# GpSimd in written order, and transposes of r, v and x moved from TensorE to the DMA crossbar from tile 10 on

## The chip, the cores and the metric

The kernel runs on one core of a Trainium2 chip. The metric is the device time of one execution in microseconds (us). The fast executions of one kernel on one core agree within about 1.5 per cent here, so each comparison below is of medians over several runs, taken beside runs of the kernel before on the same chip.

## The reference

A linear recurrence per head (seq 768, 8 heads of 40, batch 4), followed by a mixing block. Cut to what matters:

```python
for t in range(S):                       # the recurrence
    y[t]  = r[t] @ state
    Sa    = state @ a[t]
    state = state * w[t] - outer(Sa, b[t]) + outer(v[t], k[t])
# x = y as (batch, seq, 320)
theta  = x @ w_theta
zr, zi = x * cos(theta), x * sin(theta)
u      = x + w_tok_r @ zr + w_tok_i @ zi
out    = u + relu(u @ w_ch)
```

Inputs and output are float32. The kernel works in chunks ("tiles") of 128 time steps: 24 tiles, 6 per batch entry, numbered 0 to 23.

## The kernel before: the parts that matter

The loop is software-pipelined. Step i computes the recurrence of tile i, while tile i+4 is loaded, i+2 is prepared and i+1 is scored; theta of tile i-1 is made in the same step. Each tile has six loads of 160 KB, all issued from SyncE (SP).

```python
for dst, ap in ((q.w, w), (q.kb[:, 0], k), (q.kb[:, 1], b),
                (q.a, a), (q.rv[:, 0], r), (q.rv[:, 1], v)):
    nc.sync.dma_start(out=dst, in_=src(ap))                    # load(i)

# prep_rv: cast r and v to bf16, one after the other
nc.gpsimd.tensor_copy(out=q.rvb[:, j, :, 0:D], in_=q.rv[:, j])
# prep_csi: k and b times invW;   prep_cse: a times Wi (the tile ah)
nc.gpsimd.tensor_tensor(out=q.kbh[:, j, :, 0:D], in0=q.kb[:, j], in1=q.invW[:, 0], op=ALU.mult)

def tr_rv(i):                            # eight 128x128 transposes on TensorE, one copy out of PSUM
    q = tiles[i]
    pt = tile_of(ps_sm, [128, 1024], BF16, "sm")
    transpose4(pt[:, 0:512], q.rvb[:, 0])
    transpose4(pt[:, 512:1024], q.rvb[:, 1])
    q.rvT = tile_of(trs, [128, 2, 512], BF16, "rvT")
    evac(out=q.rvT.rearrange("p a b -> p (a b)"), in_=pt)

def out_xt(i):                           # three transposes of x, for theta
    tiles[i].xT = x_transpose(x_t[i % (2 * NCH)], f"xT{i % NCH}")

for i in range(N):
    nxt(load, i + 4)
    ...                                  # recurrence of tile i
    if i > 0:
        out_y(i - 1)                     # writes x of tile i-1
    nxt(prep_csi, i + 2)
    nxt(prep_cse, i + 2)
    ...
    if i > 0:
        out_xt(i - 1)
    ...
    nxt(prep_rv, i + 2)
    for m in yrows:
        moe_y(*m)
    nxt(tr_rv, i + 2)
    if i > 0:
        moe_theta(i - 1)                 # reads xT of tile i-1
    sc_lams(i, i + 1)                    # reads rvT of tiles i and i+1
```

The order in the source isn't the order on the engines: a scheduler orders each engine's instructions by what it reckons will be ready first, and leaves in written order only those that are marked with `keep_in_program_order`. The orders are fixed when the program is built. In the kernel before, GpSimd's casts and products and SP's DMAs aren't marked.

Of the kernel before, what the change touches and what calls it, by code (L numbers as in the profile page):

```python
# [10 lines left out]
BF16 = mybir.dt.bfloat16  # L11
AF = mybir.ActivationFunctionType
ALU = mybir.AluOpType
# [5 lines left out]
def kernel(  # L19
# [14 lines left out]
    nc = tc.nc  # L34
    B, H, S, D = r.shape
    C = 128
    NCH = S // C
    DM = H * D
# [21 lines left out]
    nc.vector.memset(pi2_col, math.pi / 2)  # L60

    NB = 4

    def padded(name, shape, n, pads):
        ts = [consts.tile(shape, BF16, name=f"{name}_{i}") for i in range(n)]
        for i, t in enumerate(ts):
            to_zero.append((i, pads(t)))
        return ts
# [7 lines left out]
    ah_t = padded("ah", [128, H, 64], 2, last24)  # L76
    kb_t = padded("kb", [128, 2, H, 64], NB, last24)
    rv_t = padded("rv", [128, 2, H, 64], NB, last24)
    nu_t = padded("nu", [128, H, 64], 2, last24)
    gt_t = padded("gt", [128, G, 2, 64], 2, last24)  # L80
    x_t = padded("x", [128, 3 * 128], 2 * NCH, lambda t: t[:, DM:])
# [6 lines left out]
    trs = ctx.enter_context(tc.tile_pool(name="trs", bufs=3))  # L88
    scs = ctx.enter_context(tc.tile_pool(name="scs", bufs=2))
    sml = ctx.enter_context(tc.tile_pool(name="sml", bufs=2))  # L90
    xp = ctx.enter_context(tc.tile_pool(name="xp", bufs=2))
# [8 lines left out]
    def evac(out, in_):  # L100
        if busy_act[0]:
            nc.vector.tensor_copy(out=out, in_=in_)  # L102
        else:
            nc.scalar.copy(out=out, in_=in_)  # L104
# [4 lines left out]
    def tile_of(pool, shape, dt, tag):  # L109
        return pool.tile(shape, dt, name=tag, tag=tag)  # L110
# [3 lines left out]

    tiles = [T() for _ in range(B * NCH)]

    def load(i):
        q = tiles[i]
        bi, ci = divmod(i, NCH)

        def src(ap):
            return ap[bi, :, ci * C:(ci + 1) * C, :].rearrange("h t d -> t h d")
        q.w = tile_of(raw, [128, H, D], FP32, "raw_w")
        q.a = tile_of(raw, [128, H, D], FP32, "raw_a")
        q.kb = tile_of(raw, [128, 2, H, D], FP32, "raw_kb")
        q.rv = tile_of(raw, [128, 2, H, D], FP32, "raw_rv")
        for dst, ap in ((q.w, w), (q.kb[:, 0], k), (q.kb[:, 1], b),
                        (q.a, a), (q.rv[:, 0], r), (q.rv[:, 1], v)):
            nc.sync.dma_start(out=dst, in_=src(ap))  # L129
# [7 lines left out]
    def prep_rv(i):  # L137
        q = tiles[i]
        q.rvb = rv_t[i % NB]
        for j in range(2):  # L140
            if i < 2:
                nc.scalar.copy(out=q.rvb[:, j, :, 0:D], in_=q.rv[:, j])
            else:
                nc.gpsimd.tensor_copy(out=q.rvb[:, j, :, 0:D], in_=q.rv[:, j])

    reload = [False]

    def prep_csi(i):
        q = tiles[i]
        csi = tile_of(ps_sm, [128, 512], FP32, "sm")  # L150
        nc.tensor.matmul(csi[:, 0:DM], lhsT=ntri_inc, rhs=q.lw[:, :, 0:D],
                         start=True, stop=True)
        if reload[0]:
            ln_exp_again()
            reload[0] = False
        q.invW = tile_of(exps, [128, 1, H, D], FP32, "invW")
        tc.keep_in_program_order(nc.scalar.activation(  # L157
            out=q.invW.rearrange("p o h d -> p (o h d)"), in_=csi[:, 0:DM],
            func=AF.Exp))
        q.kbh = kb_t[i % NB]  # L160
        for j in range(2):
            (nc.vector if i < 2 else nc.gpsimd).tensor_tensor(  # L162
                out=q.kbh[:, j, :, 0:D], in0=q.kb[:, j], in1=q.invW[:, 0],
                op=ALU.mult)

    def prep_cse(i):
        q = tiles[i]
        cse = tile_of(ps_sm, [128, 512], FP32, "sm")
        nc.tensor.matmul(cse[:, 0:DM], lhsT=tri_exc, rhs=q.lw[:, :, 0:D],
                         start=True, stop=True)  # L170
        nc.tensor.matmul(cse[:, DM:DM + 8], lhsT=ident,
                         rhs=off_diag.rearrange("p g c -> p (g c)"),
                         start=True, stop=False, skip_group_check=True)
        for g in range(G):
            nc.tensor.matmul(cse[:, DM + 2 * g:DM + 2 * g + 2],
                             lhsT=q.lw[:, 2 * g:2 * g + 2, :].rearrange(
                                 "p a b -> p (a b)"),
                             rhs=ones2, start=False, stop=True,
                             skip_group_check=True)
        q.Wi = tile_of(exps, [128, DM + 8], FP32, "Wi")  # L180
        tc.keep_in_program_order(nc.scalar.activation(
            out=q.Wi, in_=cse[:, 0:DM + 8], func=AF.Exp))
        q.ah = ah_t[i % 2]
        (nc.vector if i < 2 else nc.gpsimd).tensor_tensor(
            out=q.ah[:, :, 0:D], in0=q.a,
            in1=q.Wi[:, 0:DM].rearrange("p (h d) -> p h d", h=H), op=ALU.mult)

    def transpose4(dst, src):
        for g in range(G):
            nc.tensor.transpose(out=dst[:, g * 128:(g + 1) * 128],  # L190
                                in_=src[:, 2 * g:2 * g + 2, :].rearrange(
                                    "p a b -> p (a b)"),
                                identity=ident)
# [15 lines left out]

    def tr_rv(i):  # L210
        q = tiles[i]
        pt = tile_of(ps_sm, [128, 1024], BF16, "sm")
        transpose4(pt[:, 0:512], q.rvb[:, 0])
        transpose4(pt[:, 512:1024], q.rvb[:, 1])
        q.rvT = tile_of(trs, [128, 2, 512], BF16, "rvT")
        evac(out=q.rvT.rearrange("p a b -> p (a b)"), in_=pt)
# [117 lines left out]
    def out_nut(i):  # L334
        q = tiles[i]
        pt = tile_of(ps_sm, [128, 1024], BF16, "sm")
        transpose4(pt[:, 0:512], q.nu)
        q.nuT = tile_of(trs, [128, 512], BF16, "nuT")
        nc.scalar.copy(out=q.nuT, in_=pt[:, 0:512])  # L339
# [22 lines left out]
                                op=ALU.mult)  # L362

    def out_xt(i):
        tiles[i].xT = x_transpose(x_t[i % (2 * NCH)], f"xT{i % NCH}")

    def x_transpose(src, tag):
        pt = tile_of(ps_sm, [128, 1024], BF16, "sm")
        for kt in range(3):
            nc.tensor.transpose(out=pt[:, kt * 128:kt * 128 + 128],  # L370
                                in_=src[:, kt * 128:kt * 128 + 128], identity=ident)
        dst = tile_of(xp, [128, 3, 128], BF16, tag)
        evac(out=dst.rearrange("p a b -> p (a b)"), in_=pt[:, 0:384])
        return dst
# [81 lines left out]
    def ln_exp_again():  # L456
        tc.keep_in_program_order(nc.scalar.preload_act_table_set(LN_EXP))
# [15 lines left out]
    def moe_y(bi, j):  # L473
        yp = tile_of(ps_sm, [128, 512], FP32, "sm")
        y_part(yp[:, 0:DM], bi, j, range(NT), True, True)
        y_evac(yp[:, 0:DM], bi, j)

    def moe_ut(bi, j):
        q = tiles[bi * NCH + j]
        q.uT = x_transpose(u_t[(bi * NCH + j) % 3], "uT")  # L480
# [10 lines left out]
    N = B * NCH  # L491
    nc.scalar.preload_act_table_set(LN_EXP)

    def nxt(f, i):
        if i < N:
            f(i)
# [7 lines left out]
    for i in range(4):  # L504
        load(i)
# [19 lines left out]
    for i in range(N):  # L525
        bi, ci = divmod(i, NCH)
        yrows = rows_at.get(i, [])
        sines = ci == 4 or (ci == 1 and bi > 0)
        nxt(load, i + 4)
        rec_x0(i)  # L530
        nxt(tr_a, i + 1)
        nxt(tr_kb, i + 1)
        rec_nu(i)
        if i > 0:
            out_y(i - 1)
        nxt(prep_csi, i + 2)
        nxt(prep_cse, i + 2)
        nxt(sc_psiphi, i + 1)
        out_nut(i)
        rec_gt(i)  # L540
        nxt(ev_phi, i + 1)
        if i > 0:
            out_xt(i - 1)
        nxt(prep_ln, i + 3)
        if sines:
            due = (bi, (0, 1, 2)) if ci == 4 else (bi - 1, (3, 4, 5))
            moe_sines(*due)
            z_due += [(due, m) for m in range(3)]
            reload[0] = True
            busy_act[0] = True  # L550
        for m in prev:
            moe_ch(*m)
        nxt(prep_rv, i + 2)
        for m in yrows:
            moe_y(*m)
        nxt(tr_rv, i + 2)
        if i > 0:
            moe_theta(i - 1)
        sc_lams(i, i + 1)
        rec_gd(i)  # L560
        for m in yrows:
            moe_ut(*m)
        busy_act[0] = False
        if i == 0:
            moe_weights()
        if 3 <= i < NCH + 3:
            wtok_load(i - 3)
        if 6 <= i < NCH + 6:
            wtok_trans(i - 6)
        for e in z_due[:1 if ci not in (2, 3) and i < N - 1 else 3]:  # L570
            moe_z(*e)
            z_due.remove(e)
        prev = yrows
# [59 lines left out]
```

## Time and profile before

| | before |
|---|---|
| time, median of 3 runs | 247.59 us (245.44 to 248.49) |
| profiled span, mean granted TensorE clock | 244.9 us, 0.967 |
| step 12 to 21, mean | 8.36 us |
| DMA moved | 30.81 MB |

Two groups of lines of the page of the kernel before are needed beside those that the prediction shows. They are the busy time of the engines with its share of the span and the number of instructions, and the DMA queue of SP with packets, MB and the share of the 16 engines' time.

```profile
PE 206.4 (84%) x3368; PEld 161.5 (66%) x3368; DVE 188.4 (77%) x289; ACT 157.7 (64%) x301; POOL 119.7 (49%) x184
...
q1 hardware_dynamic: 153216, 27.54, 62.2%
```

TensorE (PE) is the fullest engine, and VectorE (DVE) comes next. SP's queue already takes 62% of the 16 DMA engines' time, most of it in the first 130 us, where the slices of the page show the DMA at 9 tenths.

### The profile page before, as it was taken

To read this page: it belongs to the slowest core of one execution; us is meant where nothing else is said; L and a number is where in the kernel's file an instruction comes from. 1 tells how busy PE (TensorE), PEld (TensorE's weight loads), DVE (VectorE), ACT (ScalarE), POOL (GpSimd) and SP (SyncE) were. 2 spreads that over 40 slices of the span, in tenths; PEclk is the share of its full clock that TensorE was granted. 3 is DMA by queue.
4 is the path that set the end of the run, shared out by engine and by line. 5 is a ranking of instruction groups with operands and counts; after the bars stand their busy time and mean duration, and the time that the engine had idled before them with its cause. 6 is when DMAs were issued, how large, how long until landed. Compare 5 with 4: busy or idle time off the path is not lost.

```text
span 244.9 us, 8109 instructions
## 1 busy us (share of the span) xinstructions
PE 206.4 (84%) x3368; PEld 161.5 (66%) x3368; DVE 188.4 (77%) x289; ACT 157.7 (64%) x301; POOL 119.7 (49%) x184
## 2 busy tenths in 40 slices
PE   1476899974299699989999999989999999989992
PEld 0354578753277588767787778777877778666750
DVE  6387799987069979898889978997899878755063
ACT  2394677896056885687668866887688737625230
POOL 3009556537558759356545835584447340514100
PEclk9999999999569979999999999999999999999997
DMA  7999998999999999999979987654100000111012
GB/s 132 175 190 155 172 186 146 181 191 181 174 186 176 177 189 165 158 157 181 183 147 172 169 164 127 128 111 96 44 4 31 27 29 3 54 56 54 3 53 107
DMA packets 155684, 30.81 MB, mean 126 GB/s; under 512 B 150400, under 2 KB 155648, under 8 KB 155648
## 3 DMA queue, kind: packets, MB, share of 16 engines
q1 hardware_dynamic: 153216, 27.54, 62.2%
q0 software_dynamic: 2432, 2.77, 7.4%
q8 instruction: 26, 0.43, 0.8%
q14 instruction: 10, 0.08, 0.1%
HBM read 29.13 MB, written 3.93 MB: 135 GB/s over the span
## 4 chain that ended last, share of the span: by engine, by line
PE 52%; ACT 12%; DMA 10%; DVE 7%; POOL 7%; issue 6%; SPq 5%; POOLq 0%; ACTq 0%; DVEq 0%
PE sm L463 11%; PE sm L190 9%; PE sc L222 7%; PE sm L418 6%; SPq L129 5%; DMA raw_rv<-in_v_dram 5%; DVE lamu L230 3%; ACT cs L453 3%; DMA raw_rv<-in_r_dram 2%; DVE lamv L230 2%; PE sm L370 2%; PE sc L463 2%; PE sm L357 2%; ACT L453 2%; DMA raw_kb<-in_k_dram 2%
## 5 line engine op out<-in xcount | busy, mean ns | idle before, releaser
L230 DVE TENSOR_TENSOR lamv<-sc,mask_p 128x1024 bf16<-128x1024 f32 x24 | 29.3, 1223 | 9.7 <-PE sc L222 9.5
L230 DVE TENSOR_TENSOR psi<-sc,mask_p 128x1024 bf16<-128x1024 f32 x24 | 29.4, 1224 | 5.4 <-PE sc L222 4.8
L463 PE MATMUL sm<-zi,wtok_i 128*128 128x320 bf16 x120 | 33.1, 299 | 0.0
L463 PE MATMUL sm<-zr,wtok_r 128*128 128x320 bf16 x120 | 33.1, 299 | 0.0
L104 ACT COPY rvT<-sm 128x1024 bf16<-128x1024 bf16 x18 | 18.2, 1011 | 19.1 <-PE sm L190 19.0
L230 DVE TENSOR_TENSOR lamu<-sc,mask_p 128x1024 bf16<-128x1024 f32 x24 | 29.2, 1215 | 0.3 <-PE sc L222 0.3
L230 DVE TENSOR_TENSOR phi<-sc,mask_n 128x1024 bf16<-128x1024 f32 x24 | 29.1, 1214 | 0.0
L162 POOL TENSOR_TENSOR kb_92<-raw_kb,invW 128x320 bf16<-128x320 f32 x12 | 10.1, 865 | 26.0 <-ACT invW L157 26.0
L201 DVE COPY kbT<-sm 128x1024 bf16<-128x1024 bf16 x24 | 16.4, 683 | 8.0 <-PE sm L190 8.0
L208 ACT COPY aT<-sm 128x512 bf16<-128x512 bf16 x24 | 14.2, 590 | 9.2 <-PE sm L190 8.7
L339 ACT COPY nuT<-sm 128x512 bf16<-128x512 bf16 x24 | 14.1, 587 | 9.0 <-PE sm L190 9.0
L463 PEld LDWEIGHTS <-wtok_r 128*128 128x128 bf16 x144 | 14.0, 98 | 6.0 <-issue 0.8
L463 PEld LDWEIGHTS <-wtok_i 128*128 128x128 bf16 x144 | 14.0, 97 | 5.6
L222 PE MATMUL sc<-aT,kbT 64*128 64x128 bf16 x384 | 16.1, 229 | 0.0
L357 PEld LDWEIGHTS <-lamu 128*128 128x128 bf16 x192 | 13.4, 98 | 3.2 <-DVE lamu L230 3.1
L162 POOL TENSOR_TENSOR kb_93<-raw_kb,invW 128x320 bf16<-128x320 f32 x12 | 10.1, 860 | 10.3 <-ACT invW L157 10.3
L281 ACT ACTIVATE nx<-sm 128x320 bf16<-128x320 f32 x24 | 10.7, 444 | 6.4 <-PE sm L277 6.3
L432 ACT COPY th<-sm 128x320 f32<-128x320 f32 x24 | 10.3, 429 | 6.5 <-PE sm L418 6.4
L354 PEld LDWEIGHTS <-lamv 128*128 128x128 bf16 x192 | 14.0, 97 | 0.6 <-issue 0.5
L418 PE MATMUL sm<-wch,uT 128*128 128x320 bf16 x72 | 13.4, 299 | 1.2 <-ACT invW L157 0.6
L104 ACT COPY uT<-sm 128x384 bf16<-128x384 bf16 x18 | 8.5, 482 | 8.3 <-PE sm L370 8.3
L347 PE MATMUL sm<-gd,rvT 128*128 128x80 bf16 x80 | 13.1, 200 | 0.4 <-DVE gd L102 0.4
(334 smaller groups left out, 664.2 us busy)
## 6 DMA issues: line engine op xcount, KB each, us to landing
raw_w<-in_w_dram SPq DMA_DIRECT2D x24, 160.0 KB, 3.9
raw_kb<-in_k_dram SPq DMA_DIRECT2D x24, 160.0 KB, 3.9
raw_kb<-in_b_dram SPq DMA_DIRECT2D x24, 160.0 KB, 3.9
raw_a<-in_a_dram SPq DMA_DIRECT2D x24, 160.0 KB, 4.1
raw_rv<-in_r_dram SPq DMA_DIRECT2D x24, 160.0 KB, 3.9
raw_rv<-in_v_dram SPq DMA_DIRECT2D x24, 160.0 KB, 3.9
out_dram<-oo SPq DMA_DIRECT2D x24, 160.0 KB, 1.8
wtok_row_r<-in_moe_w_tok_r_dram POOLq DMA_DIRECT2D x6, 192.0 KB, 4.2
```

What stands on the lines that cost most here:

```text
L104: nc.scalar.copy(out=out, in_=in_)
L162: (nc.vector if i < 2 else nc.gpsimd).tensor_tensor(out=q.kbh[:, j, :, 0:D], in0=q.kb[:, j], in1=q.invW[:, 0], op=ALU.mult)
L190: nc.tensor.transpose(out=dst[:, g * 128:(g + 1) * 128], in_=src[:, 2 * g:2 * g + 2, :].rearrange("p a b -> p (a b)"), identity=ident)
L201: nc.vector.tensor_copy(out=q.kbT.rearrange("p a b -> p (a b)"), in_=pt)
L208: nc.scalar.copy(out=q.aT, in_=pt[:, 0:512])
L222: nc.tensor.matmul(P[:, p, g, :], lhsT=lhs[rows(p), g * 128:(g + 1) * 128], rhs=rhs[rows(p), g * 128:(g + 1) * 128], start=True, stop=True)
L230: nc.vector.tensor_tensor(out=s.rearrange("p a b c -> p (a b) c"), in0=P.rearrange("p a b c -> p (a b) c"), in1=mask.to_broadcast([128, 2 ...
L339: nc.scalar.copy(out=q.nuT, in_=pt[:, 0:512])
L354: nc.tensor.matmul(o, lhsT=q.lamv[:, p, g, :], rhs=q.kbh[:, 0, h, 0:D], start=first, stop=False, skip_group_check=True)
L357: nc.tensor.matmul(o, lhsT=q.lamu[:, p, g, :], rhs=q.kbh[:, 1, h, 0:D], start=False, stop=True, skip_group_check=True)
L418: nc.tensor.matmul(dst, lhsT=lhs[:, kt, :], rhs=rhs[:, kt, :], start=kt == 0, stop=kt == 2)
L463: nc.tensor.matmul(yp, lhsT=wtok[nm][:, sb, j * 128:(j + 1) * 128], rhs=z[:, sb], start=start and n == 0, stop=stop and n == 2 * len(sbs) - 1)
```

## The change

The intent has two parts. GpSimd's casts and products stay in written order, so that a cast waiting for its load can't stand in front of products whose data is there. And TensorE, which bounds the steady part, loses eleven transposes a step: from tile 10 on, r and v (rvT) and x (xT) are transposed by DMA, issued from SP. Beside this, tr_rv moves from two tiles ahead to one, and the two casts of ScalarE in tiles 0 and 1 are marked to stay in written order too (cut from the diff).

```diff
+    XBAR = 10
+    def on_pool(ins, i=2):
+        if i >= 2:
+            tc.keep_in_program_order(ins)
... (prep_rv, prep_csi, prep_cse: the GpSimd instruction is wrapped in on_pool)
-                nc.gpsimd.tensor_copy(out=q.rvb[:, j, :, 0:D], in_=q.rv[:, j])
+                on_pool(nc.gpsimd.tensor_copy(out=q.rvb[:, j, :, 0:D],
+                                              in_=q.rv[:, j]))
...
     def tr_rv(i):
         q = tiles[i]
+        if i >= XBAR:
+            q.rvT = tile_of(trs, [128, 2, 512], BF16, "rvT")
+            nc.sync.dma_start_transpose(
+                out=q.rvT.rearrange("p a (g t) -> p (a g) t", t=128),
+                in_=q.rvb.rearrange("p a h d -> p (a h d)"))
+            return
...
     def out_xt(i):
+        if XBAR <= i < N - 1:
+            tiles[i].xT = tile_of(xp, [128, 3, 128], BF16, f"xT{i % NCH}")
+            nc.sync.dma_start_transpose(out=tiles[i].xT, in_=x_t[i % (2 * NCH)])
+            return
...
+        if 2 <= i + 1 < N:
+            tr_rv(i + 1)
         for m in prev:
             moe_ch(*m)
         nxt(prep_rv, i + 2)
         for m in yrows:
             moe_y(*m)
-        nxt(tr_rv, i + 2)
```

More of the change, by code (lines that the diff above doesn't have):

```diff
@@ L141, in prep_rv @@
             if i < 2:
-                nc.scalar.copy(out=q.rvb[:, j, :, 0:D], in_=q.rv[:, j])
-            else:
-                nc.gpsimd.tensor_copy(out=q.rvb[:, j, :, 0:D], in_=q.rv[:, j])
+                tc.keep_in_program_order(
+                    nc.scalar.copy(out=q.rvb[:, j, :, 0:D], in_=q.rv[:, j]))
+            else:
+                on_pool(nc.gpsimd.tensor_copy(out=q.rvb[:, j, :, 0:D],
+                                              in_=q.rv[:, j]))
     reload = [False]
@@ L161, in prep_csi @@
         for j in range(2):
-            (nc.vector if i < 2 else nc.gpsimd).tensor_tensor(
+            on_pool((nc.vector if i < 2 else nc.gpsimd).tensor_tensor(
                 out=q.kbh[:, j, :, 0:D], in0=q.kb[:, j], in1=q.invW[:, 0],
-                op=ALU.mult)
+                op=ALU.mult), i)
     def prep_cse(i):
@@ L183, in prep_cse @@
         q.ah = ah_t[i % 2]
-        (nc.vector if i < 2 else nc.gpsimd).tensor_tensor(
+        on_pool((nc.vector if i < 2 else nc.gpsimd).tensor_tensor(
             out=q.ah[:, :, 0:D], in0=q.a,
-            in1=q.Wi[:, 0:DM].rearrange("p (h d) -> p h d", h=H), op=ALU.mult)
+            in1=q.Wi[:, 0:DM].rearrange("p (h d) -> p h d", h=H), op=ALU.mult), i)
     def transpose4(dst, src):
```

## The prediction

> **What bounds the kernel now.** I read the slices of the page first, then busy time by stretches, then the waits and the chain of waits around the one large hole, then the timeline of the steady part. The slices (40 of 6.1 us each) split the run:
>
> ```profile
> PE   1476899974299699989999999989999999989992
> PEclk9999999999569979999999999999999999999997
> DMA  7999998999999999999979987654100000111012
> ```
>
> DMA is full up to about 130 us and idle after 165. PE has one hole in the 11th slice (59 to 66 us); in the slices next to it the granted clock is 5 and 6 tenths. From 83 us on PE is full. Two stretches matter:
>
> ```profile
> 59.00:66.00 7.00, 0.40 (x4) 0.40 (x5) 1.39 (x2) 0.25 (x1) 4.30 (x7) 0.66 1.04 179
> 119.30:194.50 75.20, 72.56 (x1248) 58.00 (x1249) 67.21 (x92) 57.67 (x110) 42.38 (x60) 1.00 0.56 107
> ```
>
> The columns are length, then busy us of PE, weight loads, VectorE, ScalarE, GpSimd, then clock, DMA share, GB/s. In the first, nothing runs but GpSimd and the DMA. The second is nine steps of the loop (the negated x, nx, of tile 12 starts at 119.3, that of tile 21 at 194.5), so 8.36 us a step. PE is busy 72.56 of 75.20 and VectorE 67.21: **PE bounds this part, VectorE is next with 7.47 us a step**, ScalarE needs 6.4 and GpSimd 4.7.
>
> The hole is made by GpSimd's order. Its timeline there:
>
> ```profile
> 54.44 0.45 POOL L144 CAST rv_97<-raw_rv 128x320 bf16<-128x320 f32 x1 [3.72 <-DMA raw_rv<-in_r_dram]
> ...
> 62.65 0.45 POOL L144 CAST rv_94<-raw_rv 128x320 bf16<-128x320 f32 x1 [2.64 <-DMA raw_rv<-in_r_dram]
> 63.06 1.67 POOL L162 TENSOR_TENSOR kb_93<-raw_kb,invW 128x320 bf16<-128x320 f32 x2
> 64.69 0.86 POOL L184 TENSOR_TENSOR ah_89<-raw_a,Wi 128x320 bf16<-128x320 f32 x1
> ```
>
> The longest wait of PE in the view of waits (total, times, longest):
>
> ```profile
> PE sm L190 <- POOL ah_89 L184: 6.9, 1, 6.9
> ```
>
> Buffers go by tile number modulo 4, so rv_94 belongs to tile 8 and kb_93 to tile 7. The scheduler had placed the cast of r of tile **8** ahead of k, b and a of tile **7**, and that cast waited for its load until 62.65. What tile 7 needed had long been there: its invW was computed at 55.55 and its Wi at 55.89 (ScalarE's timeline), and its a was the load issued just before its r, whose cast began at 54.44. PE asked for ah of tile 7 from 58.7 and got it at 65.6.
>
> **What the Trainium skill says.** "TensorE: Matmul & The Clock Gate", Part 1, says that an idle window of about 3.4 us brings TensorE's clock to half and that sustained work brings it back. The trace agrees: after the 6.9 us hole the clock reads 0.84 over 66 to 83 us. "VectorE: DVE Perf Modes", section The three transpose paths, gives 390 ns for a 128x128 bf16 transpose on TensorE and 1309 ns by the DMA crossbar. The first is the time of one alone: in this trace eight in a row cost 56 ns each (below). "DMA: Bandwidth & Descriptors", Latency and other measured facts, gives 261 GB/s for a DMA transpose with a non-contiguous middle dimension and 350 to 400 when contiguous; no run so far shows one. Its section Issuing engines are not separate DMA queues says that all DMAs interleave on the same 16 engines; here loads of 160 KB take 3.9 us to land although one is issued every 0.8 us or so, hence some five are in flight, and a transpose issued in the full stage joins that queue.
>
> **The change, part by part.**
>
> *1. GpSimd in written order.* In each step this is k and b times invW, a times Wi, the casts of r and v of the same tile, then DMA issues and the products with cos and sin. This is also the order in which SP issues the loads (w, k, b, a, r, v), so a cast that waits for its load holds back only work whose data comes later still. No work is added. For tile 7: its k, b and a products could start when invW is there, 56.0, and take 1.67 + 0.82 = 2.5 us, so ah is ready at about 58.5, just when PE asks (58.7). The hole of 6.9 us closes. Tile 6 shows the same in small: its casts of rv waited until 46.13, its products came at 48.20, and PE's timeline has a gap of some 1.8 us there. The clock: 17 us at 0.84 instead of 1.0 are up to 2.7 us of lost array time, of which perhaps half lies on the path. The sum is 6.9 + 1.8 + 1.3 = 10. Against this, the DMA is full there and sets a new floor: a of tile 8 is issued at 54.90 and lands some 4 us later, so tile 8's products can end at about 61.5, where they now end at 71.4. The next loads come every 7 us or so, faster than a step of 8. So the loads don't take the gain back, but each part of it has to pass through steps that are no longer idle. I take **8 us**.
>
> *2. r and v transposed by DMA, tiles 10 to 23 (14 tiles).* PE loses eight transposes a tile. Their price is read from one row of the steady part:
>
> ```profile
> 174.90 0.61 PE L190 MATMUL sm<-ident,rv_94 128*128 128x128 bf16 x8
> ...
> L104 ACT COPY rvT<-sm 128x1024 bf16<-128x1024 bf16 x18 | 18.2, 1011 | 19.1 <-PE sm L190 19.0
> ```
>
> The last of the eight takes its modelled 0.22, so (0.61 - 0.22) / 7 = 0.056 us each, and 8 x 0.056 = 0.45 us a tile. The copy out of PSUM disappears with it: 1.01 us of ScalarE, or 0.69 of VectorE in the six that fall beside the sines.
>
> *3. x transposed by DMA, tiles 10 to 22 (13 tiles).* Three transposes, 3 x 0.056 = 0.17 us of PE, and a ScalarE copy of 0.48 us.
>
> Together PE gets 0.62 us a step, ScalarE 1.5 us, and one PSUM buffer of the four is asked for twice less often. Steps 9 to 22, some 13 steps: 13 x 0.62 = 8 us at most. VectorE's floor of 7.47 us (about 7.3 without its share of the rvT copies) stops a step at 0.9 to 1.0 us below today's 8.36, so it does not forbid the 0.62, but it gets close, and the chain of a step also passes over ScalarE and VectorE. I count 0.45 us for 13 steps, **6 us**.
>
> *4. What it costs.* 14 x 256 KB + 13 x 96 KB = 4.8 MB of extra transfer; at the skill's 261 GB/s an estimate of 19 us of full DMA, against loads that run short of work from 130 us on. The time to landing matters more. For rvT there is room: the cast comes a whole step before its scores. For xT there is little: x of tile 17 is written at 171.55 to 172.04 and its theta product starts at 175.34, so 3.3 us. After 130 us an unhindered DMA fits (stores here land in 1.8 us). In steps 11 to 14 the queue is full and a landing of 4 to 6 us would leave PE waiting 1 to 2 us a step, unless the schedule puts theta later. SP also issues in order: a transpose that waits for its cast or its x holds back the loads behind it, but by then the loads run two to three tiles ahead. I charge **2 us** in all.
>
> *5. tr_rv one step later.* For tiles 2 to 9, PE transposes r and v of the next tile, not of the one after. That asks for data a step later, good while the DMA is full, but PE may wait for the 1.01 us copy before the scores. I count it as zero.
>
> Sum: -8 - 6 + 2 = -12 us, so 247.6 - 12 = 235.6; I say **235**.
>
> **The rivals.**
>
> *A. The DMA transposes are slow or queue up.* If a 256 KB transpose takes 8 us or more to land, or holds SP's queue for several us, rvT misses its step and PE waits in every step from 10 on; 2 us times 13 would eat everything and the time would be 245 to 260. For it: the skill's 1309 ns for a single 32 KB block, which for eight blocks one after the other would be 10 us; the full DMA up to 130 us. Against it: the bandwidth that the skill gives, and that the change waits for tile 10, when the loads are ahead.
>
> *B. VectorE becomes the bound at once.* The four masked evictions of 1.22 us, the kbT copy and the small ones fill 89% of the step. If the step's chain runs through them, PE's 0.62 us turn into waiting for scores, and part 2 and 3 give 1 or 2 us instead of 6: about 240. For it: from 119 to 200 us lamv waited 7 times for scores, 0.7 us each, and psi 6 times, 0.15 each, so VectorE is rarely starved. Against it: in the steady part PE, not VectorE, is the fuller one.
>
> *C. The hole closes but the DMA-bound front takes the gain back.* Then part 1 gives 2 to 3 us and the total is about 240. Against it: at 116 us r of tile 16 has landed while the products of tile 13 are only just being made, so the loads have three tiles in hand.
>
> *D. More than the sum.* With ScalarE 1.5 us a step freer and PSUM freer, small waits vanish too, and the step falls to 7.6: 10 us there, about 228 in all.
>
> **Range and chances.** A is 10%, B and C together 30%, D 15%, the rest near the sum. The limit for faster by over 2% is 247.6 x 0.98 = 242.6. Half the expected gain passes it; only A, or B and C at once, fail it. The range that should hold it 8 times in 10 is 228 to 243. Faster 0.80, same 0.13, slower 0.07.
>
> **What the profile after would show.** Part 1: no wait of PE for ah of several us, no slice under 9 in PE at 59 to 66 us, a clock of 0.95 or more over 66 to 83 us, and nx of tile 12 at about 110 instead of 119. Parts 2 and 3: PE's transposes of rv and x gone from tile 10, ScalarE's rvT copies down from 18 to about 7, steps of about 7.9 us from tile 12 to 21. A: transposes with a median of over 6 us to landing and PE waiting for rvT or xT. B: VectorE at over 95% in the steady part. C: casts and products on GpSimd waiting for loads at 60 to 110 us. The prediction is most likely wrong through the price of a DMA transpose, which nothing in this trace shows.

## The result

The changed kernel is correct and slower: **258.98 us** (257.87 to 261.27, 4 runs) against 246.61 (245.44 to 248.49, 4 runs with the earlier three). A ratio in this document is the mean time of one kernel's fast runs over that of the other's fast runs of the same rounds, so it isn't quite the ratio of the medians. Here it is 1.0506, with a 95% interval of 1.0399 to 1.0613. Executions over 1.5% slower than the fastest of the same kernel are left out of the means. The granted clock is 0.967 in both profiles.

The slices of the changed kernel are 6.4 us each:

```profile
PE   2678699858869914984897778877979899989992
...
PEclk9999999999999975999799999999999999999997
DMA  8999989999999999999968988998933133202012
```

The hole of before (11th slice) is gone. A new one, with TensorE's clock down to 5 tenths, stands in the 15th and 16th slices, at 90 to 103 us, and the steady part that was all nines is now full of sevens and eights. The DMA stays at 8 or 9 tenths until 186 us instead of 130. The busy time by stretches, with the columns length, then busy us of PE, weight loads, VectorE, ScalarE, GpSimd, then clock, DMA share and GB/s:

```profile
59.00:66.00 7.00, 6.41 (x127) 4.88 (x126) 6.22 (x8) 4.72 (x11) 6.55 (x12) 1.00 1.07 174
83.00:119.00 36.00, 24.34 (x399) 19.68 (x393) 23.72 (x33) 16.29 (x32) 14.89 (x23) 0.86 1.05 177
125.90:165.00 39.10, 32.10 (x555) 24.86 (x554) 30.14 (x42) 21.93 (x45) 19.28 (x28) 0.98 0.88 157
```

From 59 to 66 us TensorE is busy 6.41 us where it was busy 0.40 before. From 83 to 119 it is busy only 24.34 of 36, and afterwards 32.1 of 39.1. The waits (total, times, longest) name what TensorE waits for, and in the first line how ScalarE in turn waits for TensorE's theta:

```profile
ACT th L449 <- PE sm L435: 37.2, 13, 5.4
...
PE sm L435 <- DMA xT<-x: 16.1, 10, 4.1
...
PE sc L235 <- DMA rvT<-rv: 9.3, 1, 9.3
```

L435 is the product of theta and L235 the scores. TensorE now waits once, for 9.3 us, for a transposed r and v, and ten times, for 16.1 us in all, for a transposed x.

The starts of the steps (each by its nx, the negated x of the recurrence) divide the difference of the two profiled spans, 256.7 - 244.9 = +11.8 us:

| stretch | before, us | after, us | difference |
|---|---|---|---|
| start to step 9 | 92.0 | 84.3 | -7.7 |
| step 9 to 10 | 8.6 | 19.2 | +10.6 |
| step 10 to 12 | 18.7 | 22.4 | +3.7 |
| step 12 to 21 | 75.2 | 81.7 | +6.5 |
| step 21 to the end | 50.4 | 49.1 | -1.3 |

So the changed kernel was 7.7 us ahead when the first crossbar transpose was needed, and lost 20.8 us in the twelve steps after that.

**The wait at tile 10.** The timeline of the changed kernel across engines (start, length, instruction):

```profile
82.34 0.90 SPq L134 DMA_DIRECT2D raw_w<-in_w_dram  x1
82.55 0.85 POOL L150 CAST rv<-raw_rv 128x320 bf16<-128x320 f32 x2
83.34 2.11 SPq L134 DMA_DIRECT2D raw_kb<-in_k_dram  x1
...
89.93 0.57 PE L435 MATMUL sm<-wth,xT 128*128 128x320 bf16 x3
...
91.04 0.68 SPq L134 DMA_DIRECT2D raw_w<-in_w_dram  x1
...
95.19 0.79 SPq L134 DMA_DIRECT2D raw_rv<-in_v_dram  x1
96.16 1.47 SPq L221 DMA_TRANSPOSE rvT<-rv  x1
...
99.77 0.50 PE L235 MATMUL sc<-rvT 64*128 64x128 bf16 x6 [9.27 <-DMA rvT<-rv]
```

The cast of r and v of tile 10 ended at 83.40. SP, at that moment, was at the first load of tile 12. In SP's fixed order the transpose comes after all loads of tiles 12 and 13, so it was issued at 96.16, 12.8 us after its source was ready. It landed 3.6 us later. The transfer is the small part of the wait; the place in the queue is the large one.

**The waits for xT.** One later step in the same view:

```profile
174.44 0.49 DVE L374 TENSOR_TENSOR x<-sm,Wi 128x320 bf16<-128x320 f32 x1
...
175.27 1.23 SPq L380 DMA_TRANSPOSE xT<-x  x1
...
179.36 0.58 PE L435 MATMUL sm<-wth,xT 128*128 128x320 bf16 x3 [1.73 <-DMA xT<-x]
```

Here SP is prompt (x is written at 174.93, the issue comes at 175.27), but the transposed x lands only at 179.32, 4.05 us after issue, and TensorE had asked for it at 177.6. The lines on DMA issues (`--dma`) give the medians from issue to landing:

```profile
rvT<-rv SPq DMA_TRANSPOSE x14, 3.3
xT<-x SPq DMA_TRANSPOSE x13, 3.7
```

Without these waits the nine steps from 12 to 21 would have taken some (81.7 - 12.0) / 9 = 7.74 us each (12.0 of the 16.1 us of waits fall there; an estimate, as other waits could have come in their place), against 8.36 before. The relief of TensorE is therefore there; it is more than paid back in waits.

### The profile page after: what moved, and what is told of

Read it like the earlier page. It is cut to its first block, busy times and chain, and to the rows that moved or that the text cites. A ratio compares the mean times of both kernels' runs of the same rounds, so it can differ in the third digit from the quotient of the medians.

```text
span 256.7 us, 7818 instructions
## 1 busy us (share of the span) xinstructions
PE 199.3 (78%) x3217; PEld 153.9 (60%) x3217; DVE 184.9 (72%) x285; ACT 142.7 (56%) x278; POOL 119.3 (46%) x184
## 4 chain that ended last, share of the span: by engine, by line
PE 37%; DMA 26%; DVE 12%; ACT 8%; SPq 7%; issue 5%; POOL 3%; DVEq 0%; ACTq 0%; POOLq 0%
DMA xT<-x 15%; PE sc L235 7%; SPq L134 7%; DMA raw_w<-in_w_dram 7%; PE sm L480 6%; PE sm L197 5%; DVE lamu L243 5%; PE sm L435 4%; DVE lamv L243 3%; PE sm L370 2%; PE sc L480 2%; DMA raw_rv<-in_v_dram 2%; ACT cs L470 1%; DVE psi L243 1%; ACT rvT L105 1%
## 5 line engine op out<-in xcount | busy, mean ns | idle before, releaser
L169 POOL TENSOR_TENSOR kb<-raw_kb,invW 128x320 bf16<-128x320 f32 x44 | 37.1, 865 | 91.6 <-ACT invW L164 91.6
L458 POOL TENSOR_TENSOR zr<-cs,x 128x320 bf16<-128x320 f32 x22 | 17.8, 810 | 23.6 <-ACT cs L470 23.5
L435 PE MATMUL sm<-wth,xT 128*128 128x320 bf16 x72 | 14.0, 301 | 18.2 <-DMA xT<-x 16.1
L235 PE MATMUL sc<-rvT 64*128 64x128 bf16 x192 | 10.1, 225 | 14.2 <-DMA rvT<-rv 9.3
L458 POOL TENSOR_TENSOR zi<-cs,x 128x320 bf16<-128x320 f32 x24 | 19.0, 794 | 3.4 <-ACT cs L470 2.8
L435 PEld LDWEIGHTS <-xT 128*128 128x128 bf16 x72 | 5.6, 97 | 24.2 <-DMA xT<-x 19.4
L191 POOL TENSOR_TENSOR ah<-raw_a,Wi 128x320 bf16<-128x320 f32 x22 | 19.0, 862 | 0.0
L150 POOL CAST rv<-raw_rv 128x320 bf16<-128x320 f32 x44 | 18.7, 453 | 0.1
L197 PE MATMUL sm<-ident,kb 128*128 128x128 bf16 x192 | 16.0, 230 | 3.5 <-ACT nx L294 1.6
L235 PEld LDWEIGHTS <-rvT 64*128 64x128 bf16 x192 | 5.7, 96 | 19.3 <-DMA rvT<-rv 9.6
L367 PE MATMUL sm<-kb,lamv 128*128 128x40 bf16 x192 | 16.7, 180 | 0.0
```

The source lines that it names most:

```text
L150: on_pool(nc.gpsimd.tensor_copy(out=q.rvb[:, j, :, 0:D], in_=q.rv[:, j]))
L169: on_pool((nc.vector if i < 2 else nc.gpsimd).tensor_tensor(out=q.kbh[:, j, :, 0:D], in0=q.kb[:, j], in1=q.invW[:, 0], op=ALU.mult), i)
L191: on_pool((nc.vector if i < 2 else nc.gpsimd).tensor_tensor(out=q.ah[:, :, 0:D], in0=q.a, in1=q.Wi[:, 0:DM].rearrange("p (h d) -> p h d", ...
L197: nc.tensor.transpose(out=dst[:, g * 128:(g + 1) * 128], in_=src[:, 2 * g:2 * g + 2, :].rearrange("p a b -> p (a b)"), identity=ident)
L235: nc.tensor.matmul(P[:, p, g, :], lhsT=lhs[rows(p), g * 128:(g + 1) * 128], rhs=rhs[rows(p), g * 128:(g + 1) * 128], start=True, stop=True)
L367: nc.tensor.matmul(o, lhsT=q.lamv[:, p, g, :], rhs=q.kbh[:, 0, h, 0:D], start=first, stop=False, skip_group_check=True)
```

## The experiments

The theory after reading the traces: the order of GpSimd gives what was predicted; the crossbar costs more than it gives, because its transposes queue on SP behind loads and because xT is needed sooner than it lands. The rivals are that the transfers themselves, in the full DMA, are too much, or that another engine should issue them. The runs in one table (median of before in the same rounds: 246.6 to 248.8):

| run | what it is | median us | ratio, 95% interval | step 12 to 20, us |
|---|---|---|---|---|
| before | | 247 | 1 | 8.28 |
| after | the change | 258.98 | 1.0506, 1.0399 to 1.0613 | 9.06 |
| e1_order | order and shift of tr_rv, no crossbar | 241.70 | 0.9751, 0.9677 to 0.9824 | 8.30 |
| e9_order_only | order alone | 254.88 | 1.0269, 1.0204 to 1.0334 | 8.54 |
| e17_shift_only | shift alone | 248.05 | 1.0025, 0.9999 to 1.0052 | 8.27 |
| e13_no_order | crossbar and shift, no order | 265.40 | 1.0708, 1.0630 to 1.0786 | 9.25 |
| e2_rv | change without x | 247.38 | 0.9971, 0.9901 to 1.0041 | 8.00 |
| e3_x | change without r and v | 249.47 | 1.0060, 0.9986 to 1.0134 | 8.07 |
| e4_from14 | change from tile 14 | 247.15 | 0.9988, 0.9898 to 1.0078 | 9.36 |
| e7_act | e2, issued from ScalarE | 277.03 | 1.1175, 1.1063 to 1.1287 | 10.43 |
| e8_act_theta | all from ScalarE, theta later | 266.30 | 1.0775, 1.0695 to 1.0855 | 9.27 |
| e6_theta | change, theta later | 249.74 | 1.0109, 1.0024 to 1.0194 | 8.50 |
| e5_keep | e2, SP's order mended | 240.37 | 0.9715, 0.9656 to 0.9775 | 8.00 |
| e11_keep14 | e5 from tile 14 | 238.35 | 0.9606, 0.9556 to 0.9656 | 8.06 |
| **e18_keep12** | e5 from tile 12 | **237.18** | 0.9590, 0.9532 to 0.9648 | 7.99 |
| e14_keepall_late | change, SP's order mended, theta later | 247.62 | 1.0004, 0.9935 to 1.0073 | 9.18 |
| e16_rv_loads_pool | e14, two loads a tile from GpSimd | 245.90 | 0.9946, 0.9923 to 0.9969 | 8.59 |
| e19_fewer_loads | e14, two loads a tile fewer (wrong result) | 234.98 | 0.9486, 0.9399 to 0.9574 | 7.61 |

All but the last give the reference's result.

### The parts alone

**e1_order**, the order and the shift without the crossbar:

```diff
-    XBAR = 10
+    XBAR = 99
```

> GpSimd in written order and tr_rv one step later, no crossbar transpose at all. Theory (the order is a gain, the crossbar transposes lose it again through waits of PE): about 238 us (236 to 241), hole at 59 to 66 us closed, no wait of PE over 3 us. Rival (the order or the later tr_rv costs the time): 250 or more.

It took 241.7 us, ratio 0.9751: a gain, though the interval doesn't settle whether it is over 2%. The first stretch of its trace, in the columns of before:

```profile
59.00:66.00 7.00, 5.86 (x114) 4.54 (x113) 5.37 (x7) 4.71 (x11) 7.00 (x12) 1.00 0.99 169
```

The hole is closed (PE 5.86 of 7.00), and step 12 starts at 112.0 instead of 119.3. Of these 7.3 us some 6 are left at the end by the medians, and 4.4 between the two profiled spans (240.5 against 244.9): the stretch from step 21 on is about 2.8 us longer (53.2 against 50.4). The steps in between take 8.30 us, as before.

**e2_rv** and **e3_x** have the order and one half of the crossbar each. e2 turns off the crossbar for x, e3 that for r and v:

```diff
-        if XBAR <= i < N - 1:        # out_xt, e2_rv
+        if False:
-        if i >= XBAR:                # tr_rv, e3_x
+        if False:
```

> The change with only r and v transposed by DMA, x on PE. Theory (two separate losses: one wait of 9.4 us for rvT of tile 10, whose transpose stands in SP's queue behind all six loads of tile 13, and some 16 us of waits for xT): the wait at tile 10 stays (8 to 10 us), those for xT go, 241 to 246 us. Rival (the DMA traffic of the transposes slows everything): 252 or more.

> The change with only x transposed by DMA, r and v on PE. Theory: no wait at tile 10, but PE waits 1 to 3 us for xT in nearly every step, 245 to 251 us. Rival (xT waits are only a by-product of the queue that the rv transposes make): xT waits under 0.7 us a step and 240 or less.

The waits of e2_rv (first fence) and of e3_x (second):

```profile
PE sc L235 <- DMA rvT<-rv: 8.5, 1, 8.5
```

```profile
PE sm L435 <- DMA xT<-x: 10.5, 1, 10.5
```

Each half has one long wait, at its first tile. In e3_x the wait for each xT that was expected didn't come: after the first, xT landed in 2.3 to 3.2 us up to tile 20, and in 3.8 and 3.6 us at the last two, where nothing waited. Its first xT was ready at 106.73 and was issued only at 117.12, behind the loads again. So, in these runs, the steady xT waits appear only where both kinds of transposes are on the queue, while the one long wait needs only SP's order. In both runs the steps from 12 to 20 are shorter than before (8.00 and 8.07 against 8.28): the relief of TensorE is there, and the one wait eats it together with the gain of the order.

**e4_from14** does the whole change from tile 14 on.

```diff
-    XBAR = 10
+    XBAR = 14
```

> The whole change, from tile 14 instead of 10. Theory (the 9.4 us wait comes from SP being behind with the loads while the DMA is full): by tile 14 the same holds less, so the wait for the first rvT is under 4 us; the xT waits of 1 to 2 us a step stay for 9 tiles: 246 to 251. Rival (the first crossbar transpose costs its 9 us wherever it stands): a wait of 9 us for rvT of tile 14, 255 or more.

It took 247.15 us. The wait for the first rvT shrank to 2.6 us, but that for the first xT was 5.1 us (ready at 141.06, issued at 146.15) and three more followed. A later start helps r and v; it doesn't cure x.

### The order and the shift

**e9_order_only** takes away the shift of tr_rv from e1_order:

```diff
-        if 2 <= i + 1 < N:
-            tr_rv(i + 1)
         for m in prev:
             moe_ch(*m)
         nxt(prep_rv, i + 2)
         for m in yrows:
             moe_y(*m)
+        nxt(tr_rv, i + 2)
```

> GpSimd in written order alone, with tr_rv at its old place (two tiles ahead, after the y part). My fifth step counted the shift of tr_rv as zero: then 241 to 243 us, as the run with order and shift (241.7). Rival: the shift is what cost the 1.7 us at the end of that run, then 239.5 to 240.5; or it gave part of the gain, then 244 or more.

This was a surprise: 254.88 us, 13 us more than with the shift and 7 us more than before. Its timeline in one step:

```profile
67.06 1.69 POOL L169 TENSOR_TENSOR kb<-raw_kb,invW 128x320 bf16<-128x320 f32 x2 [1.01 <-ACT invW L164]
68.65 0.33 PE L387 MATMUL sm<-ident,x 128*128 128x128 bf16 x3
68.70 0.85 POOL L191 TENSOR_TENSOR ah<-raw_a,Wi 128x320 bf16<-128x320 f32 x1
69.51 0.84 POOL L150 CAST rv<-raw_rv 128x320 bf16<-128x320 f32 x2
70.01 0.79 PE L197 MATMUL sm<-ident,rv 128*128 128x128 bf16 x8 [1.03 <-POOL rv L150]
```

In written order the casts of r and v come last of GpSimd's work on a tile, after the products with invW and Wi, and TensorE transposes them at once: it stands still for a microsecond or two a step, 14.5 us in all. The shift moves this transposing a step later, when the casts have long been made.

**e17_shift_only** is the missing corner: the shift without the order (`on_pool` does nothing, no crossbar).

> The shift of tr_rv alone, with neither GpSimd's order nor the crossbar: the fourth corner beside before (about 247.7), order alone (254.9) and both (241.7). Theory: the two parts only work as a pair; order alone makes PE stand 1 to 2.5 us a step for casts of r and v, which the shift takes away, while the shift alone leaves the hole of GpSimd's order: a hole of 6 to 9 us for ah of tile 7 stays and the time is 246 to 251. Rival (the shift by itself is the gain, the order only costs): 238 to 242.

It took 248.05 us, the time of before; the old hole is still there:

```profile
PE sm L195 <- POOL ah L189: 10.2, 3, 8.9
```

So the order costs 7 us alone, the shift gives nothing alone (0.8 us more than before, not clear of noise), and together they give 6: the two parts work only as a pair.

**e13_no_order** has the crossbar and the shift, without the order.

```diff
     def on_pool(ins, i=2):
-        if i >= 2:
-            tc.keep_in_program_order(ins)
+        pass
```

(In this run and in e17_shift_only the two casts of ScalarE in tiles 0 and 1 are unmarked again too.)

> The crossbar part and the tr_rv shift without GpSimd in written order. Theory: compute then reaches tile 9 some 7 us later (about 92 instead of 84.3) while SP's loads are no later, so the first wait for rvT shrinks from 9.4 us to 1 to 3 us, the waits for xT of 1 to 4 us per step stay, and the time is 252 to 260: the order's gain of 7 us and this wait cancel each other. Rival (the first wait is the transpose's own price): it stays near 9 us and the time is 264 or more.

The wait for the first rvT was 0.6 us, as the theory had it. Without the order, compute reaches step 9 at 92.8 instead of 84.3, and SP's loads have time to get out of the way; the transpose left SP at 93.6, landed at 99.7, and was asked for at about 99:

```profile
PE sc L233 <- DMA rvT<-rv: 0.6, 1, 0.6
```

So the 9.3 us are no price of a transpose. The size of the time was missed, though: 265.4 us against the expected 252 to 260. The old hole (8.5 us) is back, and the first xT now waits 7.8 us for SP.

### Where the transposes are issued, and in which order

**e7_act** issues the transposes of r and v from ScalarE's queue, with x on TensorE; **e8_act_theta** issues both kinds there and makes theta one step later.

```diff
-            nc.sync.dma_start_transpose(
+            nc.scalar.dma_start_transpose(
```

> As e2_rv, but the rvT transposes are issued from ScalarE's queue instead of SP's. Theory: a transpose no longer stands behind loads, so no wait of PE for rvT over 2 us although the DMA is just as full: 236 to 241 us. Rival (the full DMA, not SP's order, makes the hole): the wait stays over 6 us, 245 or more.

> Both remedies: rvT and xT issued from ScalarE's queue and theta one step later. Theory: neither wait remains, the order's gain and PE's relief add up: steps of 7.6 us, 230 to 236 us. Rival (ScalarE, which waits in its queue for the cast and for x, becomes the chain): steps over 8.2 and 240 or more.

Both missed badly, at 277.03 and 266.30 us. The waits of e7_act by the engine that stood still:

```profile
ACT xT L105 <- issue: 29.2, 9, 3.5
...
ACT nx L294 <- issue: 11.5, 1, 11.5
```

ScalarE did nothing from 84.5 to 94.6, at the first transpose, and again nine times later, 3.2 us each on average. By the records it waits there for a counter that the load of w of tile 13 advances, and SP issued that load only at 90.93; it landed at 94.60. In the records the DMAs of SP and ScalarE use eight such counters, and the transpose has the same one as that load; that they are dealt out in turn, each DMA waiting for the one eight places earlier in the built order, is inferred from this and not tested. By this reading the transpose's place in that order, behind the loads, matters as much as the queue; issued from ScalarE, the same wait stops an engine that the recurrence needs. In e8_act_theta ScalarE stood 11.3 us in the same place.

**e6_theta** keeps the change on SP and makes theta one step later, so that xT has a step more to land.

```diff
+        if i > 1:
+            moe_theta(i - 2)
...
-        if i > 0:
+        if i == N - 1:
             moe_theta(i - 1)
```

> The whole change from tile 10, but theta of a tile is emitted one step later, so xT has a step of slack (xT of tile 22 on PE). Theory (PE reaches theta about 2 us before xT lands, nothing more): waits for xT under 2 us in all, steps of tile 12 to 21 fall from 9.1 to 7.5 to 7.8 us, the hole for rvT of tile 10 stays: 242 to 247 us. Rival (DMA transposes slow the steps otherwise): steps stay above 8.4, 253 or more.

It took 249.74 us, 9 less than the change but not the expected 242 to 247. The xT waits sank to 2.9 us. The first rvT wait stayed (9.7 us), and rvT waits of 0.3 to 1.3 us appeared in later steps: SP now issued transposes 3 to 7 us after their source was ready. With the deadline of xT moved, this lateness on SP shows; whether its order is the cause is tested with e14_keepall_late below.

**e5_keep** mends the order on SP for r and v alone: the transpose is written ahead of the six loads of its step, and loads and transposes are marked to stay in written order; x stays on TensorE.

```diff
+        if XBAR <= i + 1 < N:
+            tr_rv(i + 1)
         nxt(load, i + 4)
...
-            nc.sync.dma_start(out=dst, in_=src(ap))
+            tc.keep_in_program_order(nc.sync.dma_start(out=dst, in_=src(ap)))
```

> As e2_rv (only r and v by DMA, on SP's queue), but SP's order is fixed so that each rvT transpose stands ahead of the six loads of its step (six places earlier). Theory (the hole at tile 10 is time that the transpose spends behind loads in SP's queue): the transpose is issued at about 91 instead of 98 us and the wait falls from 8.5 to 3 to 5 us; 241 to 245 us. Rival (the transpose itself, or the full DMA, is slow): the wait stays at 8 to 9 us, 247.

It took 240.37 us, against 247.38 in e2_rv. The transpose left SP 8.6 us after its source instead of 12.1, and the wait is 5.0 instead of 8.5 us:

```profile
PE sc L235 <- DMA rvT<-rv: 5.0, 1, 5.0
```

It doesn't go, because SP at tile 10 is still issuing loads of tile 12. So the six places account for 3.5 of the 7 us. Another 3.0 us are there before any transpose is needed (step 9 starts at 83.8 against 86.8). e5 also keeps all loads in written order; whether that or chance gives these 3 us wasn't tested.

**e11_keep14** and **e18_keep12** are the same from tile 14 and from tile 12.

```diff
-    XBAR = 10
+    XBAR = 14        # e18_keep12: 12
```

> Order, and r and v by DMA from tile 14 on, each transpose in SP's queue kept ahead of the six loads of its step; x on TensorE. Theory (the loss is the wait behind loads in SP's one queue while compute has caught up with the loads; at tile 14 it hasn't): no wait for rvT over 1 us, steps of about 8.05 us from 14 on, so 241.7 minus 10 times 0.3 = 238.7, range 237 to 240. Rival (the transposes themselves take something from the loads or the other transfers): waits of 1 us or more per step remain, 240.5 or more.

> As the best run so far (order, r and v by DMA, transposes ahead of their step's loads on SP, x on TensorE, 238.4 from tile 14), from tile 12. Theory: at tile 12 SP is 2 to 3 us nearer to the step than at 14, where the transpose landed 4.4 us before it was needed, so no wait over 1 us, and two tiles more give 0.6 us: 237 to 239. Rival (SP is still behind there): a wait of 2 to 4 us for rvT of tile 12, 239 to 242.

They took 238.35 and 237.18 us (the 1.2 us between them lie within their spreads), and neither has a wait for an rvT from the DMA. In e18_keep12 the first transpose is ready at 100.13, issued at 104.18, landed at 107.64 and needed at 110.4. **e18_keep12 beats both kernels**, with a ratio of 0.959 to the one before. A part of the change is thus a gain: the pair of order and shift (6 us) and r and v on the crossbar (4 to 5 us more, with SP's loads kept in written order, which wasn't run alone), if the transposes stand ahead of the loads and begin when SP has caught up.

### Why the whole change still doesn't pay

**e14_keepall_late** is the whole change with both mendings: SP's order as written (rvT ahead of its step's loads, xT after them), and theta one step later (which leaves x of tile 22 on TensorE).

> The whole change with SP's order kept as written: rvT ahead of the six loads of its step, xT after them, and theta one step later. Against the run with theta later and SP's order left to the scheduler (249.7) only the order on SP differs. Theory: the wait for the first rvT is about 5 us as in the run with r and v alone (240.4), xT lands before its theta in every step, rvT waits of 0.4 to 1.4 us per step are gone, steps 7.6 to 7.9 us: 236 to 239. Rival (xT's landing time is too long by itself, or the extra 4.8 MB crowd the loads): xT or rvT waits of over 1 us in most steps, 243 or more.

It took 247.62 us, not 236 to 239. TensorE waited for xT or rvT seven times, 13.5 us in all, and transposes left SP up to 8 us after their source was ready. SP spent 66 of the 73 us from 98 to 171 us issuing, by the medians of its kinds of DMA 1.3 to 1.4 us a transpose and 0.5 to 1.0 a load. These durations contain waiting, for a source or for a free buffer: with the shortest of each kind in that stretch they would add up to 47 us. That left two causes: SP's time, or the DMA engines behind it.

**e16_rv_loads_pool** moves two loads a tile off SP, with the same bytes:

```diff
+            eng = nc.gpsimd if i >= 12 and n >= 4 else nc.sync     # n 4 and 5 are r and v
-            tc.keep_in_program_order(nc.sync.dma_start(out=dst, in_=src(ap)))
+            tc.keep_in_program_order(eng.dma_start(out=dst, in_=src(ap)))
```

> The whole change with SP's order kept and theta one step later (247.6), but the loads of r and v of the tiles from 12 on issued from GpSimd instead of SP. In the run without this, SP spent 66 of 73 us between 98 and 171 us issuing (1.2 to 1.6 us for each transpose, 0.5 to 1.4 for each load), and its transposes left 4 to 8 us after their source was ready. Theory: SP's issuing is what holds the transposes back; two loads fewer a step free it by about 1.5 us, the waits for xT of 2.4 to 2.9 us and for rvT after tile 11 mostly vanish, and the time is 239 to 243. Rival (the DMA engines or the landing itself hold them): 246 or more. GpSimd's products may come later by its own issuing, which would show as waits for kb or ah.

It took 245.90 us: 1.7 less, on the side of the rival. The xT waits went (0.5 us left), but beside the wait for the first rvT (4.4 us) two later ones came late by 2.3 and 2.7 us because they took 7.0 and 5.9 us to land. SP's time didn't fall in step with its work: loads of k and b took 1.6 us each to issue (median) instead of 0.8. The DMA shares and rates suggest why. First e14, then e16, both in their steady part:

```profile
131.90:171.00 39.10, 32.53 (x505) 24.27 (x503) 28.37 (x40) 20.78 (x42) 19.63 (x29) 0.91 1.04 170
```

```profile
132.00:166.00 34.00, 30.00 (x497) 23.95 (x494) 28.10 (x40) 20.96 (x42) 25.45 (x36) 0.95 1.02 177
```

The DMA engines are full in both (the share can read a little over 1), at 170 to 177 GB/s. A tile moves 6 x 160 KB of loads, 160 KB of stores, 256 KB of rvT and 96 KB of xT: 1472 KB, or 1.507 MB. At 177 GB/s that is 8.5 us a tile, at 170 it is 8.9. The measured steps are 8.59 us in e16 and 9.18 in e14. This agreement alone proves nothing, since in a steady stretch the rate is just the bytes of a tile over its step. But the kernel before, with its DMA full (share 0.98 to 1.10), moved 167 to 181 GB/s in the five stretches of 20 us from 20 to 120 us, and e1_order 184 from 112 to 130 us; at these rates 1.507 MB take 8.2 to 9.0 us. If the engines can't go faster, no step can be shorter; the next run tests it. (The profiled execution of e14 took 250.47 us, 2.9 above its median, so its 9.18 is on the high side.)

**e19_fewer_loads** takes bytes away instead of issuing. Tiles from 12 on load no w and no a and reuse those of tile 11. Its output is wrong, which doesn't matter for the time. SP issues as many DMAs as in e16, but a tile moves 1152 KB.

```diff
+        few = i >= 12
+        q.w = tiles[11].w if few else tile_of(raw, [128, H, D], FP32, "raw_w")
+        q.a = tiles[11].a if few else tile_of(raw, [128, H, D], FP32, "raw_a")
...
+            if not (few and (dst is q.w or dst is q.a)):
```

> Wrong result on purpose: the whole change with SP's order kept and theta one step later (247.6), but the tiles from 12 on load no w and no a of their own and use those of tile 11. SP issues as many DMAs as in the run with the r and v loads moved to GpSimd (245.9), but the DMA engines carry 320 KB a tile less: 1152 instead of 1472 KB. Theory (with the order and the crossbar together the DMA engines are the bound of this stage: 1472 KB a tile at the measured 175 GB/s are 8.6 us, the steps that were measured): steps of 7.5 to 7.9 us from tile 12 to 20, no xT or rvT wait over 1 us there, and 236 to 240 us. Rival (the fixed landing time of a transpose, or SP's order, holds them): steps over 8.2 us and 243 or more.

```profile
145.00:175.00 30.00, 28.45 (x488) 22.29 (x489) 28.07 (x39) 22.08 (x42) 19.37 (x28) 1.00 0.83 154
```

The steps fell to 7.61 us, no wait for xT was left and none for rvT after tile 10; from tile 13 on rvT landed in 3.1 to 3.2 us, as it does with no loads in flight, and the time was 234.98 us. So in the steady part of the mended whole change it is the bytes that hold the step. (Against e16, GpSimd also issues two loads fewer; that is not separated.) For the changed kernel itself the full DMA isn't the whole of xT's lateness: its last two waits for xT (0.4 and 1.0 us) come after the last load has landed at 188 us, at a DMA share of 0.13 to 0.15, and xT still took 3.3 and 4.0 us there, against 2.3 from 184 to 203 us in e3_x. Why isn't shown. The two stretches of the changed kernel:

```profile
193.00:197.00 4.00, 3.60 (x43) 2.33 (x39) 3.58 (x6) 3.58 (x6) 2.95 (x5) 1.00 0.15 29
201.00:206.00 5.00, 4.02 (x54) 2.73 (x52) 3.87 (x6) 2.30 (x5) 3.79 (x6) 1.00 0.13 26
```

The run with r and v alone, e18_keep12, also has its DMA full:

```profile
128.00:168.00 40.00, 37.72 (x650) 29.75 (x649) 35.50 (x48) 27.67 (x58) 24.82 (x36) 1.00 1.12 177
```

It moves 1376 KB a tile, 7.7 to 8.4 us at those rates, and its steps take 7.99. TensorE is nearly full too (37.72 of 40), so the two meet about here.

## Why the prediction was wrong

**Its step 1, the order, was right** for this kernel. The hole closed, the clock stayed up, step 9 came 7.7 us earlier against a predicted 8, and 6 us were left at the end of e1_order. Not seen was that this gain leans on step 5.

**Its step 5, the shift, counted as zero, hid a large term.** Order alone loses 7 us (e9_order_only), so beside the order the shift is worth 13. As both are in the change, the sum isn't harmed by this, but the attribution was wrong: the prediction gave all of the 8 us to the order.

**Its steps 2 and 3, the relief of TensorE, were right.** It counted 0.45 us a step. Without its waits the changed kernel's step is some 7.74 us against 8.36, so 0.62, just what it had worked out for TensorE before it took a part of it; e19_fewer_loads, without the waits, runs at 7.61. r and v alone give 0.3 a step (e2_rv, e5_keep).

**Its step 4, what the transposes cost, is the step that failed.** It charged 2 us "in all". The trace of the changed kernel has 9.3 us of waiting for rvT and 16.1 us for xT, 25.4 us together. Three of its sentences were wrong:

- "holds back the loads behind it, but by then the loads run two to three tiles ahead", and "for rvT there is room". The lead was as it says: when r and v of tile 10 had been cast, at 83.4, SP was at the loads of tile 12. But it is this lead that held back the transpose, and not the other way round: in the built order the transpose stood behind all loads of tiles 12 and 13, for 12.8 us. The room was read from the trace before, with the hole of GpSimd in it. There the last load of tile 13 was issued at 91.5 and step 9 began at 92.0; with the hole closed, at 95.2 and 84.3. Without the order the same wait was 0.6 us (e13_no_order), and six places earlier on SP it was 5.0 (e5_keep). The gain of step 1 and the cost of step 4 weren't independent, and the prediction added them as if they were.
- "After 130 us an unhindered DMA fits": the order alone already moves the loads later (in e1_order the DMA share is 0.81 to 0.99 from 112 to 160 us), and the transposes add 352 KB a tile, so the DMA stayed full to 186 us. The 19 us of extra DMA time were worked out, and then not laid over the stretch in which they fall. By tile, at 177 GB/s, they are 2 us on top of 6.5, and 8.5 us is longer than the step that was promised.
- "unless the schedule puts theta later": it didn't. For xT the prediction had noted 3.3 us of room and a landing of 4 to 6, and foresaw waits of 1 to 2 us in steps 11 to 14, more than the 2 us that it charged in all; waits of 0.3 to 4.1 us came at ten of the thirteen tiles, 10 to 19.

With the measured terms the sum comes out about right: -6 for order and shift, 13 steps of -0.62 from relief, +25.4 of waits, and some 2 or 3 for the clock, which read 0.86 in the 36 us around the new hole (an estimate: 36 x 0.14 = 5, and a guess that half of it is on the path). That is about +14, against +12.4 between the medians.

**Of the rivals**, A named the right class of outcome (its 245 to 260 holds the result) by a partly wrong mechanism. The transposes were not slow, with medians of 3.3 and 3.7 us to landing and not the 6 or 8 that it asks for; they queued. And rvT missed one step, not each. Rival C (the loads take the gain back) was dismissed with the same argument, the loads in hand; the gain of the order stood, but its closeness to the loads is what the crossbar then ran into. Rival B didn't occur: VectorE was busy 30.14 of 39.1 us in the steady part. D's step of 7.6 us came only where the waits were gone (7.61 in e19_fewer_loads). Two readings of the slices before were a little off and carry nothing: the clock of 5 tenths is in the hole's own slice, and the loads went on to 172 us, not 165.

**Open** is how much of e14's distance to e16 (9.18 against 8.59 us a step) is SP's issuing and how much is chance in the order of transfers, why xT takes up to 4 us to land with no loads in flight, and what keeping SP's loads in written order is worth alone.

## What to carry to other kernels

Before moving work from a full engine to DMA, add its bytes to what the DMA carries in the same stretch and divide by the rate measured there: that is a floor for the step, and a total that seems hidden over the whole run may not be hidden where it falls. A DMA that depends on compute belongs ahead of prefetches in an in-order queue, and slack read from a trace in which compute is late is gone once compute is mended: predict the second part of a change on the timeline that the first part makes. Parts of a change that touch the same chain should be tried in all corners; here the order alone, the shift alone and both together gave +7, nothing clear of noise and -6 us.

## What the Trainium skill lacked or had wrong

- "DMA: Bandwidth & Descriptors", Latency and other measured facts, gives only a bandwidth for a DMA transpose; a time from issue to landing is lacking. Here, with no loads in flight, 256 KB within the on-chip memory landed 3.1 us after issue (after 195 us in the changed kernel) and 96 KB in 2.3 us (e3_x, 184 to 203 us) to 4.0 (the changed kernel); beside loads both took 2.3 to 7.0 us. Each held SP for 1.2 us at least. The time for a single block of 32 KB that the prediction quotes isn't to be multiplied: eight blocks landed in those 3.1 us, and not in 10.
- The same page, Issuing engines are not separate DMA queues, says that issuing from several engines saves only the usually small time of issuing. That the DMAs share the same engines agrees with e16 (two loads moved to another engine, 1.7 us gained). The time of issuing isn't small here: at its shortest a transpose of 256 KB held SP for 1.2 us of the 3.1 to its landing, and in e14 the issues took 66 of 73 us on SP, waits inside them included.
- No page has, for this chip, the rate that the 16 engines reach on many short pieces at once: here 167 to 184 GB/s at a share of 1.0 or so, with 27.54 MB in 153216 packets on SP's queue, 180 bytes each.
